# The q projection of two token chunks as one Strassen pair, in a fused attention and gated-FFN kernel

## The chip, the cores and the metric

The kernel runs on one core of a Trainium2 chip. The metric is the device time of one execution in microseconds (us), as the median of several runs. Engines are called as in the profile: PE is the matmul engine (PEld its weight loads), DVE the vector engine, ACT the scalar engine, POOL and SP the two others, which here mostly issue transfers.

## The reference

One transformer layer over S = 2048 tokens of width D = 1024, all in bf16: a layer norm, a sliding local attention with dilation, its output projection, a second layer norm, and a feed-forward block whose gate is a plain product.

```python
def _A_ref(x, wqkv, wo):              # H = 32 heads of 32, W = 8, dil = 2
    q, k, v = ...(x @ wqkv)...
    idx = pos[:, None] - (jnp.arange(W) * dil)[None, :]
    kg, vg = k[:, :, idx], v[:, :, idx]       # masked where idx < 0
    logits = jnp.einsum("bhsd,bhswd->bhsw", q, kg) * Dh ** -0.5
    attn = softmax(logits)
    return (jnp.einsum("bhsw,bhswd->bhsd", attn, vg)...) @ wo

def _B_ref(x, w_gate, w_up, w_down):          # F = 3584
    return ((x @ w_gate) * (x @ w_up)) @ w_down

h = x + _A_ref(layernorm(x), wqkv, wo)
h2 = h + _B_ref(layernorm(h), w_gate, w_up, w_down)
```

## The kernel before

The tokens are cut into 4 chunks of 512 (`TC`). Every matmul of the program proper has 128 rows of contraction, 128 output rows and 512 columns; a group of 8 matmuls fills one of 8 PSUM banks with 128 x 512 results.

**Order on PE.** First q, k and v: `qkv(c, blocks)` goes over blocks of 512 columns of `w_qkv`; blocks 0 and 1 are q, 2 and 3 are k, 4 and 5 are v, and each block makes four groups. `evac_qkv` has ACT cast each group to bf16 (L344) and SP store it in HBM (`qd`, `kd`, `vd`). Chunks 0 and 1 come first, then 2 and 3. The output projection of chunk 0 (`wo_ln2(0)`, matmuls at L602) stands between blocks 3 and 4 of chunk 3. Then comes the first half of the feed-forward block for chunk 0, called FFN 1 here (`ffn1_first`: gate and up products, PE lines `pg` and `pu`), in whose middle stands the output projection of chunk 1 (`wo_norm(1)`, L578); then the same for chunk 1 (`ffn1_second`), projection 2 (`wo_adds(2, ...)`, L998), the down products of chunks 0 and 1, and so on. From there on pairs of chunks go through the Strassen-Winograd form: of a 2 x 2 block product, 7 products in place of 8, with sums of blocks of weights and of activations prepared on DVE or POOL, and with PSUM accumulating the partial sums. These sums are made in f16. So that nothing overflows, the operands are first scaled by a power of two (`Scale`: ACT sums the absolute values of a tensor piece by piece, L635; `rows` adds them up on DVE, L639 and L640; `total` has PE multiply the column by ones, L645, and DVE makes the scale and its inverse from the exponent, L647 to L654).

**Attention runs on DVE**, in the background of PE. `attention(c)` is a generator: eight products q x k of 128 x 4096 (L477), trees of sums, the maximum and its subtraction (L497), the exponential on ACT (L499), sums of it (L502 on), the products with v (L523), sums into `oD` (L534). Its result goes through HBM to `oT`, whose transfers POOL issues. `attention(c + 1)` begins when `c` is over.

**What sets the order.** The program is written out by hand; each engine works through its own list in order. `Background` decides only where in that list the steps of the generators stand: every group of matmuls calls `bg.step(GROUP_US)`, which gives credit (times `bg.rate`) to the generators, and each step costs its estimate in us; `bg.spend` takes credit away for other DVE work. No time on the chip is known to it. Weights stream through 7 buffers (`wpool`) by loads on SP; `pump` and `retire` keep count of them.

**Norm 2 of chunk 0** is in `wo_ln2`: DVE adds the bank to x (L604), takes the statistics (L183, L184) and normalizes (L192); SP transposes the rows into `lnT2_0`, which FFN 1 reads. Norm 2 of chunk 1 has the sums on ACT instead (`Norm2`, a `NormOnScalar`).

**Toward the w_down scale.** The scale of `w_down` needs the sums of its absolute values: seven pieces through a ring buffer (`abs_down`, placed as a background generator between chunk 1's q and FFN 1) and 16 pieces in `abs_blocks` (tile names `junkb`), called at projection 2. The total is the matmul of `rowbd` (L645, output `ey`) among the first down products (L944).

Of the kernel before, what the change touches and what calls it, by code (L numbers as in the profile page):

```python
# [78 lines left out]
def kernel(  # L79
# [46 lines left out]


# [72 lines left out]
    def load_x(c, what, eng):  # L200
        tiles = []
        for t in range(4):
            xt = hp.tile([128, D], BF, tag="h", name=f"{what}{c}_{t}")
            eng.dma_start(xt[:], x[bass.ds(c * TC + t * 128, 128), :])
            tiles.append(xt)
        return tiles
# [52 lines left out]
    class NormOnScalar(Norm1):  # L259
# [16 lines left out]
        def devs(self):  # L276
            nc.scalar.activation(self.nm, self.s, ACTF.Copy, scale=-1.0 / D)
            for t in range(4):
                nc.scalar.activation(self.junk[:], self.xs[t][:], ACTF.Square, bias=self.nm[:, t:t + 1],
                                     accum_out=self.ss[:, t:t + 1])  # L280
                yield "later", self.pace
            nc.scalar.activation(self.rs4[:], self.ss, ACTF.Ln, bias=eps[:], scale=1.0 / D)
            nc.scalar.activation(self.rs4[:], self.rs4[:], ACTF.Exp, scale=-0.5)
            for t in range(4):
                nc.scalar.activation(self.nb[:, t:t + 1], self.nm[:, t:t + 1], ACTF.Copy, scale=self.rs4[:, t:t + 1])
# [14 lines left out]
        def rows(self):  # L300
            for t in range(4):
                self.row(t)
                self.transpose(t)
                yield "later", self.pace

# [33 lines left out]

    qkv_in = {}  # L340

    def evac_qkv(c, m, ps):
        sg = t1k.tile([128, HB + TC], BF, tag="t1k", name=f"sg{c}_{m}")
        nc.scalar.copy(sg[:, HB:HB + TC], ps[:])  # L344
        hg = m % 8
        if m >= 8:
            nc.scalar.copy(sg[:, 0:HB], halo[:, m - 8, :])
            if c + 1 < NCH:
                nc.scalar.copy(halo[:, m - 8, :], ps[:, TC - HB:TC])
        if m < 8:  # L350
            nc.sync.dma_start(qd[c][:, 4 * hg:4 * hg + 4, :, :].rearrange("c g d s -> (g d) c s"),
                              sg[:, HB:HB + TC].rearrange("p (c s) -> p c s", c=4))
            return
        dst = (kd, vd)[m // 8 - 1][c]
        base = sg[:, 0:1]
        win = bass.AP(base.tensor, base.offset, [list(base.ap[0]), [SUB, 4], [1, SUB + HB]])
        nc.sync.dma_start(dst[:, 4 * hg:4 * hg + 4, :, :].rearrange("c g d s -> (g d) c s"), win)
# [76 lines left out]
    def qkv(c, blocks, last=False):  # L434
        for b in blocks:
            for j in range(4):
                ps = psum.tile([128, TC], F32, tag="mm", name=f"ps{c}_{b}_{j}")
                mm_group(ps, wts["qkv", b], j, lnTs[c])
                evac_qkv(c, b * 4 + j, ps)
                bg.step(GROUP_US)  # L440
            if last:
                retire()
# [5 lines left out]
    def load_qk(c):  # L448
        qD = att.tile([128, DH, SUB], BF, tag="qD", name=f"qD{c}")
        kD = att.tile([128, DH, SUB + HB], BF, tag="kD", name=f"kD{c}")  # L450
        nc.gpsimd.dma_start(qD[:], qd[c].rearrange("c g d s -> (c g) d s"))
        nc.gpsimd.dma_start(kD[:], kd[c].rearrange("c g d s -> (c g) d s"))
        qkv_in["q", c], qkv_in["k", c] = qD, kD
# [14 lines left out]
    def attention(c):  # L468
        while c and c - 1 not in over:
            yield "later", 1.0  # L470
# [71 lines left out]
        while c + 1 < NCH and ("q", c + 1) not in qkv_in:  # L542
            yield "later", 1.0
            prefetch_qk(c + 1)
        if c + 1 < NCH:
            load_v(c + 1)
# [3 lines left out]
    class Norm2(NormOnScalar):  # L550

        what = "2_"
        pace = 0.9 * GROUP_US
# [8 lines left out]
        def finish(self):  # L562
            yield from self.devs()
            yield from self.rows()
# [4 lines left out]
    def wo_norm(c):  # L569
# [4 lines left out]
        for t in range(4):  # L574
            for hf in range(2):
# [6 lines left out]
                if hf == 0 and t > 0:  # L582
                    n.sum(t - 1)
                bg.step(GROUP_US)
        n.sum(3)
        retire(2)
        return n

    def wo_ln2(c, at={}):
        lnT = lnTp.tile([128, KO, TC], BF, tag="lnT", name=f"lnT2_{c}")  # L590
        hs = hss[c]
        mv4, rs4 = ln_tiles(f"2_{c}")

        def norm(t):
            ln = normalize(hs[t], mv4, rs4, t)
            nc.sync.dma_start_transpose(lnT[:, :, bass.ts(t, 128)], ln[:])

        for t in range(4):
            for hf in range(2):
                ps = psum.tile([128, 512], F32, tag="mm", name=f"wo{c}_{hf}_{t}")  # L600
                for kk in range(KO):
                    nc.tensor.matmul(ps[:], lhsT=oTs[c][:, kk, t, :], rhs=wts["wo", c, hf][:, kk, :],  # L602
                                     start=(kk == 0), stop=(kk == KO - 1))
                nc.vector.tensor_tensor(hs[t][:, bass.ts(hf, 512)], ps[:], hs[t][:, bass.ts(hf, 512)], ALU.add)  # L604
                if hf == 1:
                    stats(hs[t], mv4, t)
                    rstd_of(mv4, rs4, t, t + 1)
                    bg.spend(1.5)
                elif t > 0:
                    norm(t - 1)  # L610
                    bg.spend(0.55)
                bg.spend(0.7)
                if 2 * t + hf in at:
                    at[2 * t + hf]()
                bg.step(GROUP_US)
        norm(3)
        retire(2)
        for t in range(4):
            rows = hsd[c][:, t, :]
            nc.sync.dma_start(rows, hs[t][:, D - rows.shape[-1]:D])  # L620
        return lnT, hs

    ones = const.tile([128, 128], BF)
    nc.vector.memset(ones[:], 1.0)

    class Scale:
        def __init__(self, name, n):
            self.name, self.n = name, n  # L630
            self.l1 = const.tile([128, n], F32, name="l1" + name)
            self.rowb = const.tile([128, 1], BF, name="rowb" + name)

        def add(self, k, src, junk):
            nc.scalar.activation(junk, src, ACTF.Abs, accum_out=self.l1[:, k:k + 1])  # L635

        def rows(self):
            row = small.tile([128, 1], F32, tag="l1row", name="row" + self.name)
            nc.vector.tensor_reduce(row[:], self.l1[:], mybir.AxisListType.X, ALU.add)  # L639
            nc.vector.tensor_copy(self.rowb[:], row[:])  # L640

        def total(self, ps=None):
            n = TC if ps else 64
            ps = ps or psum.tile([128, TC], F32, tag="mm", name="l1ps" + self.name)
            nc.tensor.matmul(ps[:, 0:n], lhsT=ones[:], rhs=self.rowb[:].to_broadcast((128, n)), start=True, stop=True)  # L645
            tot = const.tile([128, 1], F32, name="tot" + self.name)
            nc.vector.tensor_copy(tot[:], ps[:, 0:1])  # L647
            eb = const.tile([128, 1], I32, name="eb" + self.name)
            nc.vector.tensor_scalar(eb[:], tot[:].bitcast(I32), 0x7F800000, None, ALU.bitwise_and)
            nc.vector.tensor_scalar(eb[:], eb[:], float(27 << 23), None, ALU.max)  # L650
            sb = const.tile([128, 1], I32, name="sb" + self.name)
            nc.vector.tensor_scalar(sb[:], eb[:], -1.0, float(266 << 23), ALU.mult, ALU.add)
            ib = const.tile([128, 1], I32, name="ib" + self.name)
            nc.vector.tensor_scalar(ib[:], eb[:], float(12 << 23), None, ALU.subtract)  # L654
            self.s, self.inv = sb[:].bitcast(F32), ib[:].bitcast(F32)
# [8 lines left out]
    def abs_down():  # L664
# [11 lines left out]
        for p in range(7):  # L676
# [3 lines left out]
            yield "later", 4.9 * GROUP_US  # L680
# [55 lines left out]
    def ffn1_second(lnT, at):  # L736
# [17 lines left out]
        for b in range(7):  # L754
            if b == 5:
                hss[2] = load_x(2, "h", nc.sync)
            if b == 6:
                bg.spend(4.0)
# [116 lines left out]
    qkv(0, range(1, 4))  # L875
    load_qk(0)
    bg.finish(rows2)
    for t in range(4):
        norm1[2].transpose(t)
    xtiles[3] = load_x(3, "x", nc.sync)  # L880
    pump(6)
    state["live"] += 1
    bg.add(norm1[3].sums(), bg.now + 18.0)
    start_attention(0)
    sums = abs_down()
    bg.add(sums, bg.now + 25.0, first=True)
    qkv(1, range(4))
    qkv(0, range(4, 6))
    load_v(0)
    bg.add(norm1[3].rows(), bg.now, first=True)  # L890
# [3 lines left out]
    qkv(2, range(6))  # L894
    start_attention(2)
    hss[0] = load_x(0, "h", nc.sync)
    qkv(3, range(4), last=True)
    bg.finish(atts[0])
    bg.rate = 1.03
    bg.spend(8.0)  # L900
    nxt = wo_ln2(0)
    qkv(3, range(4, 6), last=True)
# [3 lines left out]
    def wo_1():  # L906
        bg.finish(sums)
# [3 lines left out]
        norm2.append(n.finish())  # L911
        bg.add(norm2[1], bg.now, first=True)

    hT0 = ffn1_first(nxt[0], {(4, 2): wo_1})
    bg.finish(norm2[1])
    ffn1_second(norm2[0].lnT, {})

    def f16(ap):
        return ap.bitcast(F16)
# [137 lines left out]
    def total_h1():  # L1057
# [3 lines left out]
                4: in_turn(total_h1, lambda: pull(1)), 6: lambda: pull(1)})  # L1061
# [292 lines left out]
```

## Time and profile before

| | |
|---|---|
| median of 8 runs | 770.51 us (770.25 to 770.96) |
| profiled execution | 770.68 us, of it span 768.7 us |
| PE busy | 760.5 us (99%), 3607 matmuls in the records |
| DVE busy | 606.1 us (79%) |
| ACT busy | 512.7 us (67%) |
| POOL busy | 141.8 us (18%) |
| granted TensorE clock | 1.00 |

The chain that ended last goes through PE for 96% of the span. By stage, DVE is busy 60.5 of the 63 us from 191 to 254 and 93.2 of the 96 us from 302 to 398, and 61.8 of the 90 us at the end. A busy PE alone doesn't say that PE works at its peak, since matmuls overlap in the records; the distance between starts does.

### The profile page before, as it was taken

The page shows a single profiled execution, that of the slowest core. Times are in us where ns is not written, and L with a number is a line of the kernel's source. Part 1 is how long each engine was busy: PE and PEld are TensorE (multiplying, and loading weights), DVE is VectorE, ACT ScalarE, POOL GpSimd, SP SyncE. Part 2 cuts the span into 40 slices and gives each one's busy share as a digit, 9 for nine tenths or more (in the row PEclk, how much of TensorE's full clock was granted, in tenths as well). Part 3 has the DMA queues.
Part 4 walks back from the last instruction along what each step waited for, and adds up shares of the span by engine and source line. Part 5 has one row for each costly group of instructions (what it writes and reads, how often), then busy time and mean ns, then how long its engine had stood idle before and what let it go on. Part 6 is the DMA issues. An engine that isn't in the chain of part 4 may idle for free.

```text
span 768.7 us, 10246 instructions
## 1 busy us (share of the span) xinstructions
PE 760.5 (99%) x3607; PEld 350.2 (46%) x3663; DVE 606.1 (79%) x718; ACT 512.7 (67%) x979; POOL 141.8 (18%) x152
## 2 busy tenths in 40 slices
PE   8999999999999999999999999999999999999998
PEld 6444444444444444444444444444444444444444
DVE  5639999999899999999998997975454444568863
ACT  4648966423687398777899986736777677788240
POOL 0000000200002000020000001018778677600000
PEclk9999999999999999999999999999999999999999
DMA  8999796999966689579559448674342423730001
GB/s 275 269 261 252 205 275 148 294 296 282 310 205 217 212 296 297 171 243 327 196 186 299 137 157 284 121 199 106 80 110 55 110 75 91 256 127 29 0 29 55
DMA packets 190915, 144.85 MB, mean 188 GB/s; under 512 B 81808, under 2 KB 181136, under 8 KB 188688
## 3 DMA queue, kind: packets, MB, share of 16 engines
q1 hardware_dynamic: 180416, 116.94, 54.2%
q0 software_dynamic: 3584, 22.02, 8.3%
q10 hardware_dynamic: 6864, 5.24, 2.3%
q8 instruction: 28, 0.46, 0.3%
q14 instruction: 23, 0.19, 0.1%
HBM read 110.10 MB, written 27.26 MB: 179 GB/s over the span
## 4 chain that ended last, share of the span: by engine, by line
PE 96%; DVE 2%; DMA 1%; issue 1%; ACTq 0%; DVEq 0%
PE ps L431 21%; PE dx L944 6%; PE pz L826 6%; PE pg L431 6%; PE py L826 6%; PE pwg L431 6%; PE pwu L431 6%; PE pu L431 6%; PE px L826 6%; PE wo L998 4%; PE pv L826 3%; PE ez L944 3%; PE ey L944 3%; PE ex L944 3%; PE dy L944 3%; PE wo L602 2%
## 5 line engine op out<-in xcount | busy, mean ns | idle before, releaser
L431 PE MATMUL ps<-lnT,w_qkv 128*128 128x512 bf16 x720 | 158.7, 379 | 0.8
L431 PEld LDWEIGHTS <-w_qkv 128*128 128x128 bf16 x736 | 71.7, 98 | 86.3
L344 ACT CAST sg<-ps 128x512 bf16<-128x512 f32 x96 | 55.1, 586 | 48.0 <-PE ps L431 38.4
L477 DVE TENSOR_TENSOR prod<-qD,kD 128x4096 bf16<-128x4096 bf16 x32 | 72.2, 2285 | 12.5 <-DMA kD<-kd 12.4
L523 DVE TENSOR_TENSOR pv<-vD,at 128x4096 bf16<-128x4096 bf16 x32 | 72.4, 2285 | 0.2
L826 PEld LDWEIGHTS <-sw 128*128 128x128 f16 x448 | 43.7, 98 | 53.0 <-issue 0.2
L431 PEld LDWEIGHTS <-w_wg 128*128 128x128 bf16 x448 | 43.8, 98 | 53.0
L431 PEld LDWEIGHTS <-w_wu 128*128 128x128 bf16 x448 | 43.7, 98 | 52.9
L826 PE MATMUL px<-lnT,ws 128*128 128x512 bf16 x212 | 53.1, 379 | 0.6
L536 POOL DMA_DIRECT2D od<-oD x4 | 2.2, 542 | 276.0 <-DVE oD L534 276.0
L431 PE MATMUL pg<-lnT,w_wg 128*128 128x512 bf16 x222 | 52.7, 379 | 0.1
L431 PE MATMUL pwu<-lnT,w_wu 128*128 128x512 bf16 x219 | 52.5, 379 | 0.3
L431 PE MATMUL pwg<-lnT,w_wg 128*128 128x512 bf16 x220 | 52.5, 379 | 0.2
L431 PE MATMUL pu<-lnT,w_wu 128*128 128x512 bf16 x218 | 52.4, 379 | 0.3
L826 PEld LDWEIGHTS <-ws 128*128 128x128 f16 x336 | 32.8, 98 | 39.7
L807 POOL TENSOR_TENSOR sw<-ws 128x512 f16<-128x512 f16 x26 | 30.0, 1153 | 82.8 <-PE pv L826 49.1
L944 PEld LDWEIGHTS <-gs 128*128 128x128 f16 (+1 forms) x280 | 27.3, 98 | 33.1
L479 DVE TENSOR_TENSOR prod<-prod 128x4096 bf16<-128x4096 bf16 x16 | 36.6, 2289 | 0.4
L843 ACT COPY py<-px 128x512 f32<-128x512 f32 x28 | 16.0, 570 | 28.3 <-PE px L826 28.3
L808 POOL TENSOR_TENSOR sw<-sw,ws 128x512 f16<-128x512 f16 x26 | 30.0, 1153 | 2.0
L809 POOL TENSOR_TENSOR sw<-ws 128x512 f16<-128x512 f16 x26 | 30.0, 1153 | 0.0
L810 POOL TENSOR_TENSOR sw<-ws,sw 128x512 f16<-128x512 f16 x26 | 30.0, 1153 | 0.0
(334 smaller groups left out, 1472.8 us busy)
## 6 DMA issues: line engine op xcount, KB each, us to landing
w_wg<-in_B_w_gate_dram SPq DMA_DIRECT2D x14, 1024.0 KB, 6.9
w_wu<-in_B_w_up_dram SPq DMA_DIRECT2D x14, 1024.0 KB, 6.2
w_pair<-in_B_w_gate_dram SPq DMA_DIRECT2D x14, 512.0 KB, 4.0
w_pair<-in_B_w_up_dram SPq DMA_DIRECT2D x14, 512.0 KB, 5.3
w_wo<-in_A_wo_dram SPq DMA_DIRECT2D x6, 1024.0 KB, 7.5
w_qkv<-in_A_wqkv_dram SPq DMA_DIRECT2D x5, 1024.0 KB, 10.9
kd<-sg SPq DMA_DIRECT2D x32, 144.0 KB, 4.1
kD<-kd POOLq DMA_DIRECT2D x4, 1152.0 KB, 8.8
```

Source lines behind the costliest of these rows:

```text
L344: nc.scalar.copy(sg[:, HB:HB + TC], ps[:])
L431: nc.tensor.matmul(ps[:], lhsT=wt[:, ko, bass.ts(j, 128)], rhs=rhs[:, ko, :], start=(ko == 0), stop=(ko == KO - 1))
L477: nc.vector.tensor_tensor(prod[:, j], qD[:], kD[:, :, o:o + SUB], ALU.mult)
L479: nc.vector.tensor_tensor(prod[:, :, 0:16], prod[:, :, 0:16], prod[:, :, 16:32], ALU.add)
L523: nc.vector.tensor_tensor(pv[:, j], vD[:, :, o:o + SUB], at[:, w, None, :].to_broadcast((128, DH, SUB)), ALU.mult)
L807: eng.tensor_tensor(sw[:, i, 0], a21, a22, ALU.add)
L808: eng.tensor_tensor(sw[:, i, 1], sw[:, i, 0], a11, ALU.subtract)
L809: eng.tensor_tensor(sw[:, i, 2], a11, a21, ALU.subtract)
L810: eng.tensor_tensor(sw[:, i, 3], a12, sw[:, i, 1], ALU.subtract)
L826: nc.tensor.matmul(ps[:], lhsT=lhs[:, ko, :], rhs=rhs[:, ko, :], start=(fresh and ko == 0), stop=(ko == 3), skip_group_check=not fresh)
L944: nc.tensor.matmul(ps[:, bass.ds(lo, n)], lhsT=lhs[k][:, bass.ts(q, 128)], rhs=rhs[k][:, bass.ds(lo, n)], start=(fresh and k == 0), stop=( ...
L998: nc.tensor.matmul(ps[:], lhsT=oTs[c][:, kk, t, :], rhs=wts["wo", 2, hf][:, kk, :], start=(kk == 0), stop=(kk == KO - 1))
```

## The change

1. **q of chunks 2 and 3 as one Strassen pair.** The blocks are: rows of the weight (the two halves of the contraction), `w_qkv` blocks 0 and 1, and the two chunks. For each of four pairs of row blocks there are seven products of four matmuls, instead of eight. `q_pair(0)` and `q_pair(2)` do two of the four each, on either side of output projection 0. The weights of q are scaled and converted to f16 in place ahead of attention 0 (`q_abs`, `scale_q`, `q_convert`), their 16 sums are made there (`q_weight_sums`), the 12 sums of activations behind attention 0 (`q_row_sums`), and one more just before the pair (`q_last_sum`). q of chunk 1 is multiplied with the f16 weights too, and scaled back in its move out of PSUM.
2. **Order of q, k and v.** Chunk 1 starts with block 2; blocks 3, 0, 1 follow. The load of x of chunk 3 waits for the load of k of attention 0, and the load of q of attention 0 waits for chunk 1's transposed rows. The blocks of k and v of chunks 2 and 3 come first, then pair 0, projection 0, block 5 of chunk 3, and pair 2.
3. **Norm 2 of chunk 0** has its statistics on ACT and its rows on DVE (`row_on_vector`).
4. **Projection 1** stands at the start of block 5 of FFN 1 instead of inside block 4. `abs_down` moves into FFN 1.
5. **Pace of attention**: `bg.rate` 1.06 instead of 1.03; in the last block of `ffn1_second`, `bg.spend(8.0)` instead of 4.0. `total_h1` is called two groups later in projection 2.

```diff
+def q_product(ps, lhs, rhs, fresh):
+    for ko in range(4):
+        nc.tensor.matmul(ps[:], lhsT=lhs[:, ko, :], rhs=rhs[ko], start=(fresh and ko == 0), stop=(ko == 3),
+                         skip_group_check=not fresh)
+    bg.step(GROUP_US / 2)
...
+    for i in two:
+        xb[i] = bank("x", i)
+        q_product(xb[i], a11[i], b11, True)
+        yb[i] = bank("y", i)
+        nc.scalar.copy(yb[i][:], xb[i][:])
+    for i in two:
+        v = bank("v", i)
+        q_product(v, sw[i][0], t1, True)
+        p5[i] = room[:, i, :]
+        nc.scalar.activation(p5[i], v[:], ACTF.Copy, scale=inv)
+    if between:
+        between()
+    t3 = qsum["t3"]
+    for i in two:
+        q_product(yb[i], sw[i][1], t2, False)
+        zb[i] = bank("z", i)
+        nc.scalar.copy(zb[i][:], yb[i][:])
+    for i in two:
+        q_product(xb[i], a12[i], b21, False)
+        out_scalar(2, m0 + i, xb[i])
+        q_product(zb[i], sw[i][2], t3, False)
+        ub[i] = bank("u", i)
+        nc.scalar.copy(ub[i][:], zb[i][:])
+        out_vector(3, 4 + m0 + i, zb[i], p5[i])
+    for i in two:
+        q_product(yb[i], sw[i][3], b22, False)
+        out_vector(3, m0 + i, yb[i], p5[i])
+        q_product(ub[i], a22[i], t4, False)
+        out_scalar(2, 4 + m0 + i, ub[i])
...
+        nc.vector.scalar_tensor_tensor(sg[:, HB:HB + TC], ps[:], inv, p5, ALU.mult, ALU.add)   # out_vector
+        nc.scalar.activation(sg[:, HB:HB + TC], ps[:], ACTF.Copy, scale=inv)                   # out_scalar
...
+def q_abs(k):
+    src = wts["qkv", k // 2][:, bass.ts(k % 2, 4), :]
+    if k < 2:
+        nc.vector.tensor_reduce(scale_q.l1[:, k:k + 1], src, mybir.AxisListType.XY, ALU.add,
+                                apply_absolute_value=True)
+    else:
+        scale_q.add(k, src, att.tile([128, 4, 512], BF, tag="oT", name=f"junk_q{k}")[:])
...
+def q_convert():
+    for r in range(2):
+        wt = wts["qkv", r]
+        nc.vector.tensor_scalar(f16(wt[:]), wt[:], scale_q.s, None, ALU.mult)
...
-    qkv(0, range(1, 4))
-    load_qk(0)
+    qkv(0, [1, 2], at={(1, 1): lambda: q_abs(0), (1, 2): lambda: q_abs(2), (1, 3): lambda: q_abs(1),
+                       (2, 0): lambda: q_abs(3), (2, 2): scale_q.rows})
+    qkv(0, [3], at={(3, 2): scale_q.total, (3, 3): q_convert})
+    load_qk(0, after=lnTs[1][:, 0, TC - 1:TC])
+    start_attention(0)
+    qkv(1, [2])
     bg.finish(rows2)
+    xtiles[3] = load_x(3, "x", nc.sync, after=qkv_in["k", 0][:, 0, 0:1])
...
-    qkv(2, range(6))
-    start_attention(2)
-    hss[0] = load_x(0, "h", nc.sync)
-    qkv(3, range(4), last=True)
-    bg.finish(atts[0])
-    bg.rate = 1.03
-    bg.spend(8.0)
-    nxt = wo_ln2(0)
-    qkv(3, range(4, 6), last=True)
+    qkv(2, range(2, 6))
+    rows_q = q_row_sums()
+    bg.add(rows_q, bg.now, first=True)
+    qkv(3, [2], last=True)
...
+    q_last_sum(room_q)
+    bg.spend(bg.credit)
+    bg.rate = 1.06
+    q_pair(0, room_q)
+    retire()
+    bg.spend(1.0)
+    norm2 = [wo_norm(0)]
+    norm2.append(norm2[0].finish(norm2[0].row_on_vector, 0.5 * GROUP_US))
+    next(norm2[1])
+    bg.add(norm2[1], bg.now, first=True)
+    qkv(3, [5], js=(0, 1, 2))
+    q_pair(2, room_q, between=lambda: qkv(3, [5], js=(3,)))
+    bg.finish(norm2[1])
+    retire(4)
...
-            yield "later", 4.9 * GROUP_US
+            yield "later", 7.0 * GROUP_US
...
-                bg.spend(4.0)
+                bg.spend(8.0)
...
-    hT0 = ffn1_first(nxt[0], {(4, 2): wo_1})
+    sums = abs_down()
+    bg.add(sums, bg.now + 10.0, first=True)
+    hT0 = ffn1_first(lnT2_0, {(5, 0): wo_1})
...
-                4: in_turn(total_h1, lambda: pull(1)), 6: lambda: pull(1)})
+                4: lambda: pull(1), 6: in_turn(total_h1, lambda: pull(1))})
```

## The prediction

> **What bounds the kernel now.** I read the busy line and the chain first.
>
> ```profile
> PE 760.5 (99%) x3607; PEld 350.2 (46%) x3663; DVE 606.1 (79%) x718; ACT 512.7 (67%) x979; POOL 141.8 (18%) x152
> PE 96%; DVE 2%; DMA 1%; issue 1%; ACTq 0%; DVEq 0%
> ```
>
> PE ends the chain almost everywhere. Whether its busy time is work shows in the pieces of the chain:
>
> ```profile
> 27.48 10.74 PE ps L431 x49
> 38.27 10.74 PE ps L431 x49
> 49.06 10.74 PE ps L431 x49
> ```
>
> From one start to the next, 10.79 us for 50 matmuls (a 50th stands between two pieces): 0.2159 us each, at a granted clock of 1.00. The list of waits names 0.4 us for PE once behind the start-up. So a removed matmul is worth 0.2159 us as long as nothing else comes late. A rule of the Trainium skill speaks against reading it so: "Perfetto Trace Analysis", section "Identifying the Most-Contended Engine", says that the busy share of matmuls is a bad measure and that headroom is judged by the busy share of weight loads. That is 46% here; by it PE would have room, and the removal would bring nothing (770.7). The even step decides for me.
>
> Next, who could come late. VectorE (DVE) runs the four attentions in the background, almost without pause, from the landing of kD0:
>
> ```profile
> DVE prod L477 <- DMA kD<-kd: 12.4, 1, 12.4
> ACT lg L499 <- DVE lg L497: 4.7, 2, 3.7
> ```
> ```profile
> 136.00:381.40 245.40, 244.25 (x1116) 111.03 (x1137) 237.05 (x207) 160.07 (x303) 16.03 (x22) 1.00 0.85 262
> ```
>
> The window (span, then busy PE, PEld, DVE, ACT, POOL) goes from the end of attention 0 to attention 3's subtract of the maximum (L497). DVE is busy for 237.05 of 245.40 us; of the 8.35 us idle, 5.55 lie in six gaps over 0.25 us (0.60, 1.50, 0.53, 0.58, 1.55, 0.79), the rest between dependent operations. What hangs on its end, on ACT, DVE and PE:
>
> ```profile
> 381.44 1.06 ACT L499 ACTIVATE lg<-lg 128x1024 f32<-128x1024 f32 x1 [3.65 <-DVE lg L497]
> 402.75 1.06 ACT L635 ACTIVATE ring<-ring 128x1024 bf16<-128x1024 bf16 x1 [0.19 <-DVE ring L749]
> 403.80 1.04 ACT L635 ACTIVATE junkb<-w_dn 128x1024 bf16<-128x1024 bf16 x1
> 418.63 0.19 ACT L635 ACTIVATION_READ_ACCUMULATOR junkb<-w_dn 128x1 f32 x1
> ```
> ```profile
> 418.85 0.18 DVE L639 TENSOR_REDUCE rowd<-l1d 128x1 f32<-128x23 f32 x1 [0.44 <-ACT junkb L635]
> 419.06 0.16 DVE L640 CAST rowbd<-rowd 128x1 bf16<-128x1 f32 x1
> ```
> ```profile
> 421.48 0.38 PE L645 MATMUL ey<-rowbd,ones 128*128 128x512 bf16 x1
> ```
>
> ACT waits 3.65 us for L497. Behind the exponential it works without a gap but 0.19 us (casts of the ring, its absolute sums, 16 absolute sums of w_down) up to 418.82; then DVE makes rowd and rowbd, and PE multiplies rowbd with ones for the scale of w_down. From exponential to rowbd: 419.22 - 381.44 = 37.78 us. PE comes 421.48 - 419.22 = 2.26 us later: the margin. Since these absolute sums stand behind the exponential on ACT, nothing later on ACT can shorten it.
>
> **The change, part by part.** *Fewer matmuls.* q of chunks 2 and 3 took 2 x 8 groups of 8, 128 matmuls of 512 columns. Now 4 row blocks x 7 products x 4 = 112. 16 x 0.2159 = 3.45 us, less one 64-column matmul for q's scale, about 0.05: **3.40 us** by the streaming rate. Nothing else is taken from PE.
>
> *The scale and the f16 weights of q.* DVE gets two absolute reductions of 2048 elements, five one-column operations, two conversions in place (1.28 each, the row of L925) and 16 sums of weights (0.42, the row of L700). They stand in the 12.4 us before attention 0. The reduction has no row: from below 1.22 (L481, 2048 bf16), from above 2.45 (twice L497's 1.226 for 1024 f32); I take 2.3, as a reduction has no fast form that I see in the trace. The Trainium skill ("VectorE: DVE Perf Modes", "The perf-mode tier table") has the reduction at the slowest rate only, about 2.29 by its entry for 2048 elements; the sum would be the same, as both ends fit. The total of q's scale stands some 16 matmuls ahead of chunk 1 (38.9 us), so near 35.5; 0.9 + 2.6 + 16 x 0.42 = 10.2 makes 45.7, with the layer-norm rows between (4 x 0.5) 47.7, against 51.78: cost zero with 4 us of cover. Without it attention 0 starts late one for one. ACT gets two absolute sums (1.91 + 0.19 each) near 25 us, which push chunk 1's transposes on its queue by about 2 us. In the trace the second one was issued at 31.22, took 7.49 us beside the load of qD0 and landed at 38.71, 0.2 us before PE. The qD0 load now stands behind it; the first took 3.38 us without it. 33.2 + 3.4 = 36.6: no cost; up to 2 us if it takes the 7.49 again (40.7), and no gain, as PE streams there. The two added copies on POOL wait where nothing else is due on it (its next issue in the trace is vD0 at 87.90). The load of x of chunk 3 waits for kD0 and holds SP's queue till about 52: behind it stand w_qkv_4 and 5, the transposes of chunk 2 and the last stores of kd1. w_qkv_4 is needed at 66.8 and takes 10.9: 63, cover 4 us, if that goes, one for one. The transposes of chunk 2 are needed by PE past 110, the stores by kD1 at 88.94.
>
> *DVE behind attention 0.* Added: 12 sums of rows (0.42) 5.0, t3 (2048, between 1.15 and 1.22) 1.2, eight scalar_tensor_tensor out of PSUM (0.75, the row of L784) 6.0: 12.2. Removed with the norm of chunk 0 going to ACT: 8 x 0.68 (L183) and 4 x 0.21 (L184), 6.3. Net **+5.9 us** ahead of attention 3's L497; all other DVE work between the two points is the same in both programs' orders.
>
> *Projection 0 and norm 2 of chunk 0.* Projection 0 now ends 88 matmuls, 19.0 us, ahead of FFN 1. In the trace from its end (177) to the last landing of the transposed rows (188.43) are 11.4 us: no cost. In the pair ACT gets 12 moves of a bank (0.57 to 0.69, L843 and L848) per 14 products (12.1 us): 8 us, covered; if a product waited for the one copy ahead of it, 0.6 us in each pair, so 0 to 1.2; I take 0.
>
> *Projection 1* (oT1) stands 17 matmuls later in order, at 256.7. oD1 ended at 237.12, and the first slice landed 10.9 us later. With 5.9 of which 2.1 are taken up by the first two gaps: 240.9 + 10.9 = 251.8. No cost. The abs sums of w_down's ring moved into FFN 1 take 7 x 2.1 us of ACT where it is busy 46.3 of 63 us: fits, 0; their loads are issued on ACT's own queue. On SP the pair's 16 stores of q now stand ahead of FFN 1's next weights: the second w_up waits behind the last store, which DVE has ready some 4 us after the pair's end (187.5), 191.5; with the 6.2 of the page's issue list it lands at 197.7, needed one block and one group later (9 x 1.73) at 203.1. 0; if it takes w_qkv's 10.9, 202.4, still 0, and up to 1 us with the store's own delay.
>
> *The place where it comes together.* PE reaches the w_down total at 421.48 - 3.40 = 418.08. L497's end on DVE: 237.05 + 5.9 = 242.95 of work. Of the idle, I keep the two gaps that are attention waiting for its own exponential (0.53, 0.79) and the 2.80 between dependent operations, and let the four that wait for PE or ACT close, as PE is earlier and DVE later: 242.95 + 4.1 = 247.05, against 245.40: 1.65 us later. rowbd is then ready at 419.22 + 1.65 = 420.87, PE **waits 2.8 us**. Bounds: all 8.35 close, L497 ends at 378.9, and the wait is 0; nothing closes, 5.9 later, 425.1, the wait is 7.0. Attention 3 is thinned only from the last block of FFN 1 on, behind the exponential in the order; that relieves DVE there, but ACT's chain is not shortened by it: 0. total_h1 comes two groups of 8 later in the order, 3.45 us, and so at the same time as before, 407.0, where PE waited 0.3 us for rowbh: 0 for the end, since what PE waits there it waits less at the w_down total.
>
> Sum: -3.40 + 2.75 = -0.65 on the profiled execution of 770.68 (span 768.7 and 1.98 around it): 770.0. The median of 8 is 0.17 lower: **769.9**. Behind the wait PE is 0.65 earlier than before, so the later stages keep their margins.
>
> **Rivals.** *Full saving.* DVE takes up all of its added work, or ACT's chain is shorter: PE waits under 1.9 us at the w_down total. For it: 8.35 us idle against 5.9. Against: 2.8 of these stand between dependent operations. 770.5 - 3.4 = 767.1, to 769.0.
>
> *Backlog (slower).* DVE's gaps stay where they are, since what DVE waits for (ACT's gate copies, 1.50 and 1.55) comes late too, ACT having got the sums of norm 2 and of w_down. Then exponential 3 starts at 387.3, and the wait is 7.0: 770.5 + 3.6 = 774.1. It is slower by over 0.2% from a start of 385.2 on (418.08 + 3.40 + 1.54 = 423.0, less 37.78). Against: PE is 3.4 us earlier at the gaps that wait for it.
>
> *The change doesn't do what it says.* The products could wait on banks or the weights' sums in the pair, and 3.4 us go there: 770.5. The 16 matmuls are gone in any order.
>
> **How the numbers follow.** 0.2% is 1.5 us, about what a measurement of this kernel can tell from no change: under 769.0 is faster, over 772.0 slower. The forecast (a wait of 1.9 to 4.9) 0.42, nearly all within; full saving 0.34, faster; backlog 0.18, slower; start-up or pair waits 0.06, split between within and slower. Of the forecast 0.03 falls to faster and 0.04 to slower. Faster 0.37, same 0.38, slower 0.25 after rounding up the slower side for transfers whose margins are under 2 us. The range 767.1 to 773.2 leaves out the far end of the backlog.
>
> **What would show it.** Right: PE's only new gap over 1 us is ahead of the one matmul on rowbd; the exponential of attention 3 starts between 382 and 384, and DVE is busy for about 243 us between oD0's end and that point. Wrong: that exponential before 380.5 and no gap there (full saving); after 385 (backlog); or PE gaps at 38.9, at the pair (150 to 187) or at FFN 1's start, each a margin that I set to zero.

## The result, and the profile after

The changed kernel takes 772.81 us (median of 10 runs, 772.19 to 775.14) against 770.43 us for the kernel before (28 runs, 770.07 to 771.6): a ratio of 1.0034, interval 1.0026 to 1.0042, slower by 2.4 us. Its profiled execution took 772.44 us, span 770.6 us. PE has 16 long matmuls less to do, and waits more than that saves.

The busy line, the chain's shares and PE's list of waits (us in total, times, longest) of the changed kernel:

```profile
PE 759.0 (98%) x3592; PEld 349.8 (45%) x3648; DVE 624.7 (81%) x754; ACT 532.7 (69%) x1012; POOL 144.9 (19%) x154
PE 58%; DVE 25%; ACT 9%; issue 5%; DMA 2%; SPq 0%; DVEq 0%; ACTq 0%
```
```profile
PE ey L379 <- DVE rowbd L374: 3.0, 1, 3.0
PE pwg L489 <- ACT ring L772: 0.4, 1, 0.4
```

The chain was 96% PE. Now it goes through DVE and ACT for a third of the span: it leaves PE at the w_down total (L379 here) and runs back through ACT's absolute sums and DVE's attentions. The same instructions as in the prediction, on ACT, DVE and PE:

```profile
383.33 1.06 ACT L562 ACTIVATE lg<-lg 128x1024 f32<-128x1024 f32 x1 [4.04 <-DVE lg L560]
420.87 0.19 ACT L369 ACTIVATION_READ_ACCUMULATOR junkb<-w_dn 128x1 f32 x1
```
```profile
421.09 0.18 DVE L373 TENSOR_REDUCE rowd<-l1d 128x1 f32<-128x23 f32 x1 [2.59 <-ACT junkb L369]
421.30 0.16 DVE L374 CAST rowbd<-rowd 128x1 bf16<-128x1 f32 x1
```
```profile
421.51 0.58 PE L379 MATMUL ey<-rowbd,ones 128*128 128x512 bf16 x1 [2.98 <-DVE rowbd L374]
```

The exponential of attention 3 starts at 383.33 (before 381.44), and from it to the end of rowbd pass 38.13 us (before 37.78). PE, with 3.4 us less to do, comes early and waits, and the total starts at 421.51 us, where it stood before (421.48). What follows the wait stands in the windows (span; busy PE, PEld, DVE, ACT, POOL with counts; the clock is the number ahead of the last two):

```profile
418.00:421.60 3.60, 0.62 (x4) 0.22 (x3) 0.97 (x4) 3.60 (x9) 0.00 (x0) 0.99 0.79 253
421.60:425.20 3.60, 3.38 (x9) 1.25 (x10) 3.46 (x8) 3.60 (x4) 0.00 (x0) 0.53 0.02 5
```

PE is busy in the second window and does nine matmuls where it did seventeen: the granted clock is 0.53. The even distance between the starts of weight loads is 0.2159 us. From 22 us to the end every distance over 0.26 us stands in this table with what it exceeds 0.2159 by, but for two that all three profiles have (0.08 us near 515 and 0.25 near 719). The column "again" is a second profile of the same program, told of below:

| us lost at | before | after | again |
|---|---|---|---|
| 385, FFN 1 waits for a bank | 0 | 0.57 | 0.59 |
| 407, the total of h1 | 0.30 | 0 | 0 |
| 421.5, the total of w_down | 0 | 3.14 | 3.13 |
| 421.9 to 425.1, half rate | 0 | 1.68 | 0 |
| 449 to 465, waits for DVE's sums | 0 | 0 | 0.88 |
| 501 | 0 | 0.21 | 0 |
| sum | 0.30 | 5.60 | 4.60 |

-3.40 for the matmuls, + 5.60 - 0.30 makes +1.90: the difference of the spans (770.6 - 768.7). In the second profile the same sum gives +0.90 (769.7 - 768.7): the loss does not hang on the halved clock.

### The profile page after: what moved, and what is told of

It reads as the page before. It is cut to its first block, busy times and chain, and to the rows that moved or that the text cites. A ratio compares the mean times of both kernels' runs of the same rounds, so it can differ in the third digit from the quotient of the medians.

```text
span 770.6 us, 10295 instructions
## 1 busy us (share of the span) xinstructions
PE 759.0 (98%) x3592; PEld 349.8 (45%) x3648; DVE 624.7 (81%) x754; ACT 532.7 (69%) x1012; POOL 144.9 (19%) x154
## 4 chain that ended last, share of the span: by engine, by line
PE 58%; DVE 25%; ACT 9%; issue 5%; DMA 2%; SPq 0%; DVEq 0%; ACTq 0%
PE ps L489 16%; PE dx L1092 6%; PE pz L832 6%; PE py L832 6%; PE px L832 6%; DVE prod L540 4%; DVE pv L586 4%; PE pv L832 3%; PE dy L1092 3%; DVE prod L542 2%; PE ex L1092 2%; PE ey L1092 2%; ACT ring L369 2%; ACT junkb L369 2%; DMA b21r<-in_B_w_down_dram 2%
## 5 line engine op out<-in xcount | busy, mean ns | idle before, releaser
L489 PE MATMUL ps<-lnT,w_qkv 128*128 128x512 bf16 x595 | 131.4, 379 | 0.7
L489 PEld LDWEIGHTS <-w_qkv 128*128 128x128 bf16 (+1 forms) x608 | 59.3, 98 | 70.9
L403 ACT CAST sg<-ps 128x512 bf16<-128x512 f32 x72 | 41.6, 584 | 30.3 <-PE ps L489 24.3
L813 POOL TENSOR_TENSOR sw<-ws 128x512 f16<-128x512 f16 x26 | 30.0, 1152 | 80.2 <-PE py L832 72.9
```

The costliest lines, as they stand in the source:

```text
L489: nc.tensor.matmul(ps[:], lhsT=wt[:, ko, bass.ts(j, 128)], rhs=rhs[:, ko, :], start=(ko == 0), stop=(ko == KO - 1))
L813: eng.tensor_tensor(sw[:, i, 0], a21, a22, ALU.add)
```

## The experiments

Theory A: the chain behind attention 3's exponential makes PE wait at the total, and the wait halves the clock. Rival B: ACT is late for its own added work. Theory C came out of the runs of 1 to 3: from the landing of kD0 to the sums at 463 us DVE's list is what ends last, PE only waits for it wherever it reads its results, and a wait taken away at one place comes back at the next. L numbers are those of the changed kernel (in 5, those of that run's own kernel). Clock and gaps are read from each run's profile; all ratios are to the kernel before on the same chip. The landing of kD0 (the load of k for attention 0) is taken from the start of the first product that reads it, 0.1 us behind the landing itself.

**1. The wait filled with 14, and with 7, idle matmuls.**

```diff
+            for i in range(14):          # 7 in the second run
+                nc.tensor.matmul(ys[3][:], lhsT=ones[:], rhs=A11[i % NP], start=True, stop=True)
             scale_d.total(ys[3])
```

> Edit: 14 matmuls of 512 columns whose result nobody reads stand ahead of the w_down total, in the place where PE waited 3.1 us. Theory A (the wait stays, ended by ACT's chain behind the exponential of attention 3, and a wait of that length also halves PE's clock for some 3.6 us, 1.85 us lost): the wait is filled, no matmul behind it is at half rate, 772.8 - 1.85 = 771.0. Rival (the slow matmuls behind the wait come from their operands or from what runs beside them, not from the idle time): they stay at 0.427 us each, 772.8.

> Edit: the same with 7 matmuls, so that about 1.6 us of idle time are left ahead of the total. Theory A says nothing of the length from which the clock falls: if 1.6 us is under it, 771.0, as with 14; if not, 772.8. The rival of the run with 14: 772.8.

Measured: 772.8 us both (ratios 1.0031, 1.0019 to 1.0042, and 1.0030, 1.0019 to 1.0040). With 14 the wait at the total is 0.1 us, with 7 it is 1.62, and no matmul behind is at half rate, clock 1.00 in all six executions with 14 (the changed kernel: 0.996 to 0.998 in nine of ten): the slow matmuls came from the idle time. But the time did not fall to the 771.0 of Theory A; the changed kernel's one execution at 1.00 took 772.96 us, within the range of the others. In these two profiles kD0 landed at 54.29 and 53.87 us, not 52.34; the exponential started at 385.05 and 384.64, and the bank wait at 385 had grown to 2.18 and 1.70.

**2. The exponential later in ACT's order.**

```diff
-        yield "later", 4.0 if c == 0 else 1.5
+        yield "later", (4.0, 1.5, 1.5, 5.0)[c]
         nc.scalar.activation(lg[:], lg[:], ACTF.Exp, scale=float(DH) ** -0.5)
```

> Edit: in ACT's order the exponential of attention 3 stands two casts and one absolute sum (0.47 + 0.47 + 1.91 us) later, that is behind work that was ready while ACT waited 4.04 us for DVE; nothing else changes. Theory A: the exponential starts at 383.3 as before, the chain behind it is 2.85 us shorter, PE's wait at the total falls from 3.14 to about 0.3 us, the bank wait of 0.57 at 384.9 goes and the clock stays up: 772.8 - 2.85 - 0.57 - 1.85 = 767.5. Rival B (ACT is late for its own added work, the sums of norm 2 and of the ring of w_down, and the exponential only shows it): ACT has no room ahead of the exponential, it moves back by 2.85 us, and the time is 772 to 773.

Measured: 772.76 us (1.0033, 1.0022 to 1.0045). ACT's idle time ahead of the exponential, its start, and PE's waits:

```profile
383.22 1.06 ACT L562 ACTIVATE lg<-lg 128x1024 f32<-128x1024 f32 x1 [1.46 <-DVE lg L560]
```
```profile
PE ey L1092 <- DVE gs L1260: 2.1, 1, 2.1
...
PE ey L379 <- DVE rowbd L374: 0.7, 1, 0.7
```
```profile
463.20:466.80 3.60, 3.60 (x10) 1.20 (x11) 3.47 (x5) 0.77 (x2) 0.39 (x1) 0.55 0.73 298
```

B falls: ACT had room, the exponential did not move, its idle time went from 4.04 to 1.46. At the place it aims at, A holds: the total waits 0.86 instead of 3.14, the bank wait is gone. But 45 us later PE waits 2.3 us for DVE's f16 sums (L1260), and there the clock is halved (0.55). A wait taken away came back at the next place where PE reads from DVE, price and all, and the 767.5 that Theory A gave for the time was missed by 5.3 us.

**3. Less work on DVE: the eight p5 sums left out.**

```diff
-            nc.vector.scalar_tensor_tensor(sg[:, HB:HB + TC], ps[:], inv, p5, ALU.mult, ALU.add)
+            nc.scalar.activation(sg[:, HB:HB + TC], ps[:], ACTF.Copy, scale=inv)
```

> Edit: the eight scalar_tensor_tensor of the pair (0.75 us each on DVE) become scaled copies on ACT that leave the p5 product out, so that part of q of chunk 3 lacks one product; DVE has 6.0 us less ahead of attention 3's exponential, ACT 8 x 0.57 = 4.6 us more. Theory A (DVE's added 5.9 us is what makes the exponential late): it starts 3 to 5 us earlier, 378.5 to 380.5, no wait over 1 us at the total, clock up: 767.0 to 767.8. Rival B (ACT's own added work): the exponential doesn't move and the time stays at 772 to 774.

Measured: 772.57 us (1.0025, 1.0015 to 1.0034), the wait at the total 3.12, the exponential at 382.95, 0.38 us earlier, where kD0 had landed 0.61 earlier. These are the numbers that Rival B gave. But DVE did have less to do: from the end of attention 0 to the exponential it is busy for 235.9 of 247.1 us, in the changed kernel for 240.7 of 246.8. The 5 us went into waits of DVE, its own lines show where:

```profile
156.45 0.69 DVE L655 TENSOR_TENSOR h<-wo,h 128x512 bf16<-128x512 f32 x1 [2.05 <-issue]
158.12 0.69 DVE L655 TENSOR_TENSOR h<-wo,h 128x512 bf16<-128x512 f32 x1 [0.98 <-PE wo L653]
...
198.33 0.69 DVE L565 TENSOR_TENSOR trs<-lg 128x512 f32<-128x512 f32 x1 [2.11 <-ACT lg L562]
```

The order is written by hand: a DVE that is early stands at the adds of projection 0 until PE has them (3.0 us), and then for the exponential of attention 1, which stands behind ACT's casts in ACT's order (2.11 us; 0.79 in the changed kernel). Attention does not move up.

**4. The same, with the order moved up.** The line `bg.spend(0.75)` behind the copy is left out too.

> Edit: the run with the eight light copies on ACT (one product of part of q of chunk 3 left out), and the 0.75 us of credit that each of them cost is given back, so that attentions 1 to 3 stand 26 to 33 matmuls (6 to 7 us) earlier in the order; DVE's work is the same as in that run. Theory C: DVE doesn't wait for PE at 156 to 158 and 198 us any more, exponential 3 starts at 378 to 380, no wait over 0.5 us, 767 to 768. If DVE's list is not the bound, as the unchanged exponential of the first such run could mean: 772 to 773 again.

Measured: 773.67 us (1.0042, 1.0029 to 1.0056). The exponential comes 4 us earlier, as expected of DVE's list and against Rival B, and yet the time is worse, not the 767 to 768 of Theory C:

```profile
379.35 1.06 ACT L562 ACTIVATE lg<-lg 128x1024 f32<-128x1024 f32 x1 [7.05 <-DVE lg L560]
```
```profile
PE l1psh L379 <- ACT junkb L369: 2.0, 1, 2.0
PE pwu L489 <- ACT ring L772: 1.5, 1, 1.5
```

In ACT's order the exponential had moved up by more than in time. ACT stands 7.05 us in front of it, and the casts that free PE's banks and the sums for the totals stand behind: bank waits of 1.61, 0.66 and 0.45, then 2.37 at the total of h1, with half rate behind it. Theory C alone does not give this time. What fits the runs so far is A and C together: DVE's list sets when the exponential can run, and its place in ACT's list sets what is held meanwhile.

**5. The DVE work alone, without the Strassen pair,** in the kernel before:

```diff
+        if c == 0:
+            idle = t1k.tile([128, TC], BF, tag="t1k", name="idle")
+            for k in range(14):
+                nc.vector.tensor_tensor(idle[:], lnTs[3][:, k % 8, :], lnTs[2][:, k % 8, :], ALU.subtract)
         over.add(c)
```

> Edit: the kernel before, with 14 subtractions of 512 elements (0.42 each, 5.9 us) on DVE behind attention 0, whose result nobody reads; PE has nothing less to do. Theory C: DVE's idle time of before (8.35 us up to attention 3's exponential) takes up 4 us or so, the exponential moves by about 2 us to 383.3, and of the margin of 2.26 us at the w_down total little is left: 770.4 to 771. With no idle time to take it up: exponential at 387.3, a wait of 3.6 us at the total and a halved clock behind it: 775 to 776.

Measured: 774.86 us (1.0058, 1.0045 to 1.0070), 4.3 us for 5.9 us of DVE. The exponential starts at 385.80, 4.4 us later and not 2. PE waits elsewhere than I had it:

```profile
PE pg L431 <- DMA lnT<-ln: 2.1, 1, 2.1
PE ps L431 <- DVE h L608: 2.0, 1, 2.0
```

Norm 2 of chunk 0 is on DVE in this kernel: its adds hold banks (179 us) and its rows come late to FFN 1 (195 us). PE loses 4.6 us at these two places and so reaches the w_down total late as well, without a wait there. So the run does not show what the added DVE work alone costs at that total, nor how much of it the idle time takes up. The change had moved these off, by giving the statistics to ACT and putting projection 0 earlier; that part did its work.

**6. The row sums on POOL,** from 104 us on, with 9 and with 12 us of credit cut:

```diff
-            nc.vector.tensor_tensor(t1[k], b12[:, k, :], b11[:, k, :], ALU.subtract)
+            nc.gpsimd.tensor_tensor(t1[k], b12[:, k, :], b11[:, k, :], ALU.subtract)
...
-    bg.spend(bg.credit)
+    bg.spend(bg.credit + 9.0)      # 12.0 in the second run
```

> Edit: the 12 sums of rows are made on POOL, from 108 us on, instead of on DVE behind attention 0; attention 1 follows at once, and its credit is cut by 9 us, so that in the order its steps stand 14 to 33 matmuls (3 to 7 us) earlier than in the changed kernel. Theory C, formed from the first four runs (from the landing of kD0 to the sums at 463 us DVE's list is what ends last; PE only waits for it wherever PE reads its results, so a wait taken away at one place comes back at the next): 5.0 us less on DVE bring attention 3's exponential to 378 to 379.5, the wait at the w_down total under 0.3 us and the one near 463 too: 767.3 to 768. Theory A (only the chain behind the exponential counts) says the same for the total, but not for 463. Against both: DVE and POOL slow each other, then attention 0 or 1 gets longer and 770 to 773 stays.

> Edit: the same sums on POOL, with 12 us of credit cut, so that attention 1 to 3 stand about where they stood in the order of the changed kernel (exponential 3 within 8 matmuls). Theory C: DVE, 5.0 us ahead, now waits for PE's groups where the order makes it (as in the run with the eight light copies), and gives back part: exponential 3 at 379 to 381, the wait at the total 0 to 1 us: 767.5 to 768.5. If the order doesn't matter: the same time as with 9 us.

Measured: 790.3 us (1.0265, 1.0250 to 1.0279) and 789.32 us (1.0239, 1.0224 to 1.0253). The two engines in the first run:

```profile
105.13 3.08 POOL L923 TENSOR_TENSOR qt<-lnT,qt 128x512 f16<-128x512 bf16 x1
```
```profile
116.71 3.13 DVE L595 TENSOR_TENSOR pv<-pv 128x4096 bf16<-128x4096 bf16 x1
```
```profile
PE qz L938 <- DVE room_q L933: 14.3, 1, 14.3
```

Side by side, DVE's sums of 4096 take 3.13 instead of 2.29 us, and POOL's of 512 take 3.08 to 3.20 instead of the 1.15 of L813. Attention 0 ended at 146.6 instead of 136.5, and the last sum of the pair (room_q), which this edit leaves behind attention 1's first steps, made PE wait 14.3 us. The rival named against both theories had the cause right, at a far higher price than its 770 to 773; on Theory C the two runs say nothing. The Trainium skill ("SBUF — State Buffer", "Summary: rules for kernel authors") says that when a VectorE operation has two SBUF inputs and a GpSimd operation reads SBUF, the one issued second blocks until the first is done. Both engines start one operation per 3.16 us here, which agrees with taking turns, though the two times alone would add up to 3.44.

**7. The later exponential, and one step of attention 3 put back.**

```diff
-        yield "later", 4.0 if c == 0 else 1.5
+        yield "later", (4.0, 1.5, 1.5, 5.0)[c]
...
-                bg.spend(8.0)
+                bg.spend(6.0)
```

> Edit: the later exponential of attention 3 (as in the run with that edit alone) and bg.spend(6.0) in place of 8.0 in the last block of FFN 1, so that one step of attention 3 more stands ahead of projection 2, where DVE was idle for 2.5 us, and one less near 463 us, where PE then waited for DVE. Theory C: the exponential stays at 383.2, the wait at the total 0.5 to 0.9 us, none over 0.5 us near 463, the clock stays up all the way: 772.8 - 2.3 (wait at 3.14 now 0.8) - 0.6 (bank) - 1.85 (clock) = 768.0, faster than the kernel before. If the wait only moves once more (DVE behind everywhere): 770 to 773.

Measured: **769.72 us** (11 runs, 768.75 to 770.34; 0.9986, 0.9978 to 0.9995): 3.1 us under the changed kernel and 0.8 under the kernel before, though 1.7 over the 768.0 of Theory C. The clock is 1.00, the wait at the total 1.03, and near 461 three distances are longer by 0.1 each. DVE's idle time ahead of rowd is 0.43 us (2.47 in the run of the exponential alone, 2.59 in the changed kernel): moving one DVE step of 2.3 us to where DVE stood idle is what that run lacked.

**8. The thinning undone,** `bg.spend(4.0)` in place of 8.0.

> Edit: the thinning of attention 3 undone, bg.spend(4.0) in place of 8.0, nothing else. Theory C: the exponential and ACT's chain behind it stay; a further step of 2.3 us of attention stands on DVE ahead of the row of h1 (rowbh), which was ready just as PE came (407): PE waits 2 to 3 us there and so less at the w_down total (1 us); with the halved clock behind one of them 772.5 to 775. Theory A (only the chain of ACT): 772.8.

Measured: 773.26 us (1.0032, 1.0019 to 1.0044). The wait moves to the total of h1 (3.48 us, half rate behind it), the one at w_down's is gone, and the bank wait is 1.21. In these runs the thinning only chose which of two totals waits.

**9. The load of q of attention 0 at once,** in the changed kernel and in that of 7: `load_qk(0)` without its `after`.

> Edit: the load of q of attention 0 is issued at once, as in the kernel before, not behind chunk 1's transposes. In the changed kernel it was issued at 36.6 instead of 30.8, beside the stores of k, and kD0's issue came at 45.9 to 47.0 instead of 43.9. Theory C: kD0 lands 0.5 to 2 us earlier and all of DVE's list with it, the wait at the w_down total gets shorter by as much; but chunk 1's second transpose meets that load again (7.5 us instead of 3.1) and PE waits up to 3 us at 38.6: 771 to 774, by which of the two is larger.

> Edit: the run with the later exponential and bg.spend(6.0), and the load of q of attention 0 issued at once. Theory C: as that run, 768.0, with the waits at the total shorter by what kD0 lands earlier, less what PE waits for chunk 1's transposes at 38.6 (0 to 3 us): 767.3 to 770.5.

Measured: 774.57 us (1.0050, 1.0037 to 1.0062) and 771.03 us (1.0007, 0.9998 to 1.0016), 1.8 and 1.3 us worse than with the wait. kD0 did not land earlier but at 54.4 and 54.3, and PE waited 0.70 and 0.47 us at 39. My reading that the moved load delays k's stores is wrong; what does, in the changed start, stays open.

**10. Second profiles.**

> The changed kernel once more, unedited, for a second pair of kD0's landing and time. If the landing sets the time one for one (52.34 us and a span of 770.6 in the first profile): span = 770.6 + (landing - 52.34), within 0.5 us. If the landing has no say: span 770.6 at any landing.

> The run with 14 matmuls ahead of the total once more, unedited. Its first profile had kD0 at 54.29 us, 1.95 later than the changed kernel's, and a span of 771.7. If the clock's part is worth 1.7 us and the landing acts one for one: span = 770.6 - 1.7 + (landing - 52.34), within 0.5 us. If the clock is worth nothing: 1.7 us more than that.

> The run with the later exponential and bg.spend(6.0) once more, unedited. Its first profile had kD0 at 52.11 us, a span of 766.9, a time of 768.75 against a median of 769.72. If the landing sets the time: span = 766.9 + (landing - 52.11), within 0.5 us, and a landing near 53 in the middle execution. If it has no say, the span stays at 766.9 or varies without it.

| program | kD0 lands | exponential 3 | span | half rate |
|---|---|---|---|---|
| changed | 52.34 | 383.33 | 770.6 | 1.68 |
| changed, again | 52.44 | 383.57 | 769.7 | none |
| with 14 matmuls | 54.29 | 385.05 | 771.7 | none |
| with 14 matmuls, again | 53.66 | 384.42 | 771.2 | none |
| later exponential, 6.0 | 52.11 | 383.36 | 766.9 | none |
| the same, again | 53.53 | 384.27 | 767.9 | none |

The second profile of the changed kernel missed its expectation (769.7 against 770.7) in the most useful way: the same wait of 3.13 us, and a full clock behind it.

```profile
421.80:425.40 3.60, 3.55 (x17) 1.59 (x18) 3.46 (x8) 3.60 (x4) 0.00 (x0) 1.00 0.03 9
```

So one program can run with the halving and without; the last section shows what decides. It costs 1.68 us where it falls, and 0.9 us of span: without it PE is early again, and waits 0.88 us for DVE at 449 to 465. The landing of kD0 varies by up to 1.4 us between two executions of one program, and carries into the exponential (1.42 us later made 0.91) and into the span (1.0). In the two other pairs one for one holds to 0.5 us, which is little to go by; the run with 14 matmuls lay 1.0 above its first expectation and 0.7 under the other. At a like landing it is not faster than the changed kernel without half rate, as it should be, since its matmuls take the wait's place.

## Why the prediction was wrong

The forecast was 769.9 us and a gain of 0.65 us in the profile; the loss was 1.9 us there and 2.4 us in the medians. The time lies inside its range, the sign is wrong.

- *Fewer matmuls*, 3.40 us: right; outside the lines of the table every matmul keeps its 0.2159 us (the waits of 0.3 and 0.4 us that the list names for the kernel before all lie in the first 10 us). So the even step was the right row to go by, and the busy share of weight loads, 46%, would have misled (by it PE had room; it had none).
- *Scale and weights of q*: right. The reduction took 2.28 us (2.3), DVE was done at 48.7 (47.7), the transposes of chunk 1 landed at 34.6 and 35.8, and no wait followed. kD0 landed 0.56 us later, which I had not in the sum.
- *DVE behind attention 0*: right in sum, by luck. Exponential 3 was due at 381.44 + 1.65 = 383.1 and came at 383.33. The stretch from the end of attention 0 to it, as in the prediction:

```profile
136.50:383.30 246.80, 245.64 (x1124) 111.89 (x1144) 240.72 (x215) 184.99 (x333) 16.01 (x22) 1.00 0.85 262
```

  It begins 0.5 us later (kD0), where the sum had 0. DVE's busy time grew by 3.7 us (237.05 to 240.72), where it had 5.9. Its idle time fell by 2.3 us (8.35 to 6.08), where it had 4.25. 0.5 + 3.7 - 2.3 makes 1.9, and the three errors nearly cancel. One reason for the second: the sum adds up durations of rows, but DVE's operations overlap in the records; the 16 sums of weights of 0.42 us took 5.95 us, 0.37 each.
- *Projections 0 and 1, norm 2, the pair*: no wait at any of them, as forecast.
- *The wait at the w_down total*: right in place, cause and chain, 3.14 against 2.75 (2.79 by the prediction's own figures). rowbd was due at 420.87 and came at 421.46: 0.24 from the exponential, 0.35 from a longer chain behind it.
- *The sum* is the step that failed: "-3.40 + 2.75 = -0.65", with "Behind the wait PE is 0.65 earlier than before, so the later stages keep their margins". It took the wait at its own length and let nothing else depend on the same lateness. Measured, that term is 5.60 (5.30 more than before) and not 2.75: 0.39 for the longer wait, 1.68 for the halved clock or, without it, 0.88 at the next reads of DVE's sums, 0.57 for banks that ACT could not free while it stood 4.04 us in front of the exponential, and 0.21 at 501, whose cause stays open. I had that idle line of ACT in a fence, and followed only one of the things queued behind it.
- *Where the saving went.* The 0.57 is not what makes PE late, as the total waits for rowbd all the same: PE goes on at 421.51 us, 0.03 later than before and not 0.65 earlier, so the whole saving is gone there. Behind it the later stages do not keep their margins, and 1.68 + 0.21 (in the second profile 0.88) come on top. The thinning of attention 3, which the prediction put at 0, has a part in that: with it, once the total waited less, PE waited 2.32 us at 461 (experiment 2), and with one step put back no wait there was over 0.12 (experiment 7).
- *Backlog*, the slower rival, had the sign right for another reason: it let all 8.35 us of DVE's idle time stay, with the exponential at 387.3 and a wait of 7.0. 6.08 us stayed, the exponential came at 383.33, and it put everything on the one total.
- Open: what makes kD0 0.56 us later, and what `bg.rate` 1.06 does. No run shows either.

## What to carry to other kernels

Where a background engine's list fills its stage (DVE 237 of 245 us here), work saved on PE beside it can turn into waits (here 3.40 us saved, and none of it left behind the total), and a wait removed at one reader can appear at the next; count the whole list, at every place where PE reads from it. An instruction that waits in an in-order queue holds all that is queued behind it: two edits, of its place and of one step, were worth 3.1 us, and turned a loss of 2.4 us into a gain of 0.8. A PE wait of over 2 us should be priced at its length plus up to 1.7 us for the clock, as the next section tells.

## What the runs showed of the hardware

- A PE wait can halve the granted clock, and where the wait falls decides it. The clock records of the traces change only at whole multiples of 3.413 us from their first one (the halving of the changed kernel: 122 of them), and a half-rate stretch lasts 3.41 us, or four times that behind the waits of 14 us. So there are windows. Here are two, each with the one that follows, from the changed kernel and from the run with 14 matmuls (bank wait of 2.18 us):

```profile
418.14:421.55 3.41, 0.43 (x3) 0.14 (x2) 0.78 (x4) 3.41 (x9) 0.00 (x0) 1.00 0.79 252
421.55:424.96 3.41, 3.19 (x8) 1.18 (x9) 3.27 (x8) 3.41 (x4) 0.00 (x0) 0.50 0.02 6
```
```profile
383.07:386.48 3.41, 1.54 (x8) 0.59 (x6) 2.22 (x4) 1.43 (x3) 0.00 (x0) 1.00 1.07 378
386.48:389.90 3.42, 3.27 (x16) 1.50 (x16) 3.32 (x6) 3.42 (x6) 0.00 (x0) 1.00 0.24 90
```

  By the distances of weight loads, waits took 3.14 us of the first window shown and 2.04 of the third. From 20 us on, over all runs, the clock is halved behind every window of which waits took 2.22 us or more, and behind none of which they took 2.04 or less. The length of the wait alone does not tell: 2.32 us within one window halved it, 3.41 us in two (1.40 and 2.01) did not. The first record stands 3.9 to 6.6 us into the span, in each execution elsewhere, so the same wait can fall either way (3.14 us with, 3.13 without; the trace of the latter has no clock records, so where its windows lay is not known). One halving cost 1.3 to 1.7 us. The Trainium skill ("TensorE: Matmul & The Clock Gate", "What's actually happening") puts the fall after an idle window of about 3.4 us that runs free of the kernel: length and free running agree, but here 2.22 us of idle time in the window were enough.
- Sums of two SBUF operands on POOL (512 elements) and DVE (4096) at once take 3.08 to 3.20 and 3.13 us, against 1.15 and 2.29 alone.
- A load of 1.1 MB early in the program landed anywhere from 51.7 to 54.3 us in the 13 profiles with the changed order of loads.
